# Two-source operations for the softmax factors, and no weight pieces split by GpSimd from the last routing on

## The chip, the core and the metric

The kernel runs on one core of a Trainium2 chip. The core has five engines with a queue of instructions each: TensorE (PE; its weight loads are shown as PEld), VectorE (DVE), ScalarE (ACT), GpSimd (POOL) and SyncE (SP), which here issues most of the DMAs. Each engine takes its instructions in order, and semaphores make one engine wait for another. The metric is the device time of one execution in microseconds (us); the figure of a kernel is the median of its runs.

## The reference

Three layers follow each other in one launch, all in fp32:

```python
attn = rope_attention(q, k, v)        # 2 batches, 8 heads, 576 positions, 64 columns a head
x  = attn as [1152, 512]
p  = domain_probs / (sum + 1e-9)
x1 = sum over 4 experts e of p[:, e] * (relu(x @ w1[e]) @ w2[e])      # every expert on every token
e  = argmax of softmax(norm(x1) . norm(emb) / tau)                    # 8 experts, one per token
out[e == i] = gate * (relu(x1[e == i] @ w1b[i]) @ w2b[i])
```

The attention divides each row of exp(scores - max) by its sum + 1e-9.

## The kernel before

**Precision.** Each fp32 operand of a matmul is held as two float32r tiles, a high part "hi" (a copy that rounds) and a low part "lo" (operand minus hi); a product is three matmuls, hi hi, hi lo and lo hi. So each weight has to be split on the chip, by a copy (hi, normally ScalarE, `L657`, tile `wh`) and a subtraction with two sources in SBUF (lo, `L658`, tile `wl`).

**Attention (0 to about 190 us).** Heads go in eight pairs. `Schedule` orders the operations of all engines in a greedy run over estimated costs and ranks (`POS`), and `ENG` gives the engine of operations that have a choice. For each pair VectorE adds 1e-9 to the row sums (`row_sum`, `L350`, tile `rs`), takes the reciprocal (`L354`), and makes two operands of a small set of matmuls (`rmat`): `mrs` (`rest_factor`, `L359`) and `rb`, the factors spread over 64 columns each (`wide_factor`, `L365`). `rb` is made by GpSimd, for pair 1 by VectorE. Beside them GpSimd does the rotary products (`raw`), low parts of q and k (`n`), of v (`vs`) and of the result (`xl`), all with two sources in SBUF.

**First expert layer (190 to 585 us).** TensorE-bound; weight pieces of 128 x 512 are split between its products.

**Last routing (585 to about 622 us).** Tokens go in nine chunks of 128. `route_one` routes chunks 6, 7 and 8 one after the other: VectorE adds the last expert's sum (`L814`, tile `x`), squares it (`sq`), GpSimd takes the root (`ss`), TensorE transposes and makes the logits, VectorE picks the expert (`lm`, `eq`, `em`, `oh`, then `ss`, `nb`), ScalarE makes the gate (`ex`), and VectorE the slot (`rk`, `slot`, `es`, `seen`). `first_split` puts the 16 pieces of the first block's weights (units 0 to 3, four pieces each) between these steps: hi on ScalarE, and lo on VectorE for the six pieces named in `FIRST_ON_DVE`, on GpSimd for the other ten.

**Second expert layer (to the end).** Fourteen blocks of 128 tokens of one expert. A block has 48 matmuls of 128 x 512 (`fc1` and `fc2`, `L1291`) in four sets of 12, and 12 transposes (`turned`, `L1268`), each four of which need a copy by ScalarE and a subtraction by VectorE (`L1270`: `bxl`, `htl`). Beside them 16 weight pieces are split for the next blocks. Of each unit's four pieces the one numbered 3 has its lo on GpSimd, and for the odd units its hi on VectorE (`L655`); the rest is ScalarE and VectorE. The results leave through an indirect DMA that GpSimd issues (`L1327`).

Of the kernel before, what the change touches and what calls it, by code (L numbers as in the profile page):

```python
# [20 lines left out]
S = 576  # L21
# [7 lines left out]
class Schedule:  # L29
    """Puts operations of several engines in order: a greedy run over estimated costs, in which  # L30
    a free engine takes the operation of the lowest rank among those that can start by then."""
# [7 lines left out]
    def op(self, rank, eng, cost, f, *a, after=(), slot=None, late=0.0):  # L39
        """slot names a buffer of a ring, held from the first operation that names it until all  # L40
        in self.free[slot] are over; late is what the result takes beyond the engine's time."""
        o = dict(rank=rank, eng=eng, cost=cost, f=f, a=a, after=list(after), slot=slot, late=late, end=None)
        self.ops.append(o)
        return o

    def start(self, o, now):
        """When an operation can start, None as long as that is open."""
# [14 lines left out]
    def run(self):  # L62
        """The operations, as dicts, by their start."""
# [32 lines left out]
class Attention:  # L96
    """RoPE attention, two heads at a time; x^T goes to xh + xl (both float32r).

    Round r runs the scores and the softmax of pair r beside the transposes and the
    products with v of pair r - 1, and prepares the operands of pair r + 1.  # L100
    """
# [36 lines left out]
    # engines of the operations that have a choice, pair by pair  # L138
    ENG = {("rope", 0): "gggggggg", ("rope", 1): "gggggggg", ("rope", 2): "vvgggggg", ("split", 0): "aaaaaaaa",
           ("split", 1): "gggggggg", ("v", 0): "aaagaaaa", ("v", 1): "gggggggg", ("wide", 0): "gvgggggg",  # L140
           ("x", 0): "aaaagggg", ("x", 1): "gggggggg", ("rope1q", 0): "ggv", ("rope1k", 0): "vvv",
# [55 lines left out]
    def rope(self, eng, i, j, sl=slice(0, 2), cols=slice(0, S)):  # L197
        """Step j of x * cos + swapped x * sin, in place; slot 0 is q, 1 is k."""
# [18 lines left out]
    def spread(self, i):  # L217
        """qa = [qh; ql] of head A, qb = [ql; qh] of head B, ka and kb = k of a head on both halves."""
# [16 lines left out]
    def first_pair(self, D):  # L235
        """Loads and operands of pair 0, in small parts and without DMAs between partitions;
        what each chunk of its scores waits for."""
# [73 lines left out]
    def qk(self, i, c):  # L311
        """Scores of row chunk c; chunks 0-3 head A, 4 the rests of both, 5-8 head B."""
# [34 lines left out]
    def row_sum(self, i):  # L347
        nc, st = self.nc, self.st[i]
        rs = st["rs"] = self.p_sm.tile([128, 9], F32, name="rs")
        nc.vector.tensor_scalar(out=rs, in0=st["sum"], scalar1=1e-9, scalar2=None, op0=ALU.add)  # L350
# [5 lines left out]
    def rest_factor(self, i):  # L356
        nc, st = self.nc, self.st[i]
        mrs = st["mrs"] = self.p_sm.tile([128, 128], F32, name="mrs")
        nc.vector.tensor_scalar(out=mrs, in0=self.cst["blk"], scalar1=st["rs"][:, 8:9], scalar2=None, op0=ALU.mult)  # L359

    def wide_factor(self, eng, i):
        st = self.st[i]
        rb = st["rb"] = self.p_sm.tile([128, 8, 64], F32, name="rb")
        sh = [128, 8, 64]
        self.by(eng).tensor_tensor(out=rb, in0=self.cst["one"].unsqueeze(2).to_broadcast(sh),  # L365
                                in1=st["rs"][:, 0:8].unsqueeze(2).to_broadcast(sh), op=ALU.mult)
# [46 lines left out]
    def av(self, i, h, hf, k):  # L413
        """One of the five key chunks of x^T; any of them may come first."""
# [11 lines left out]
    def av_shift(self, i, h, hf):  # L426
        """The low half of x^T moves to the rows of the main half."""
# [12 lines left out]
    def rmat(self, i):  # L440
# [5 lines left out]
        nc.tensor.matmul(ps[:, 512:S], st["mrs"], self.cst["id2"], start=True, stop=True)  # L446
# [32 lines left out]
    def plan(self, last_round):  # L479
        """All operations, with what they wait for."""  # L480
# [14 lines left out]
        for i in range(NPAIR):  # L495
            # operands
# [34 lines left out]
            # scores and softmax  # L531
            for c in range(9):
# [11 lines left out]
            f = [op("row_factor", i, 2, "DVE", 128, self.rest_factor, i, after=[f]),  # L544
                 op("row_factor", i, 3, self.letter("wide", 0, i), 400, self.wide_factor, self.letter("wide", 0, i), i,
                    after=[f])]
            # transposes and products with v
# [57 lines left out]
class Experts:  # L605
    """Both expert layers. A weight unit is [128, 2048]: 0 and 1 are the halves of w1's columns
    as [p, k, 512], 2 and 3 the halves of w2's rows as [p, f, 512]; each is held as hi + lo."""
# [6 lines left out]
    FIRST_ON_DVE = (0, 0), (0, 1), (2, 0), (2, 1), (2, 2), (3, 0)  # L614
# [6 lines left out]
    def open_right(self, ctx):  # L621
        """Weights and the first split unit, in place of what the attention no longer needs."""
# [28 lines left out]
    def split(self, cut, u, lo_eng=None, hi_eng=None):  # L651
        nc = self.nc
        raw, hi, lo = cut(self.raw[u]), cut(self.wh[u]), cut(self.wl[u])
        if hi_eng:
            hi_eng.tensor_copy(hi, raw)  # L655
        else:
            nc.scalar.activation(out=hi, in_=raw, func=AF.Copy)  # L657
        (lo_eng or nc.vector).tensor_tensor(out=lo, in0=raw, in1=hi.bitcast(F32), op=ALU.subtract)  # L658

    def split_rows(self, u, j, *engines):  # L660
        self.split(lambda t: t[:, j * 512:(j + 1) * 512], u, *engines)

    def split_cols(self, u, j, *engines):
        self.split(lambda t: t.rearrange("p (a b) -> p a b", b=512)[:, :, j * 128:(j + 1) * 128], u, *engines)

# [18 lines left out]
    def layer1(self, xh, xl, rest):  # L684
        """All but the routing of the last token chunk, which is left in self.todo."""
        tc = self.tc
        with ExitStack() as c1:
# [28 lines left out]
            for c in range(3):  # L716
# [9 lines left out]
                # the first block's weights are split beside the chunk's routing  # L726
# [8 lines left out]
    def first_split(self, u, *js):  # L735
        for j in js:
            self.split_rows(u, j, *[] if (u, j) in self.FIRST_ON_DVE else [self.nc.gpsimd])

# [5 lines left out]
    def next_splits(self, n):  # L744
        """Splits of the weights needed next; a unit's next load follows its split."""
# [71 lines left out]

    def router_setup(self):
# [30 lines left out]
        def scale():  # L849
            """Embeddings over tau (|emb| + 1e-6)."""  # L850
# [11 lines left out]
        def empty():  # L862
            """Empty slots: zero rows whose token lies beyond the output."""
# [15 lines left out]
    def turn(self, c, cols, ps=None):  # L879
        """Part of a chunk's x1^T."""  # L880
# [27 lines left out]
    def counts(self, c, ps=None):  # L908
        """Tokens per expert in the chunks before c, in every partition."""
# [4 lines left out]
    def rank(self, cs):  # L914
        """Slots: the expert's region + tokens before in the chunk + tokens of the chunks before."""
# [8 lines left out]
    def scatter(self, c):  # L924
        # no order among the scatters can be declared between direct neighbours on the engine
# [7 lines left out]
    def route(self, chunks):  # L933
        """Logits and the one-hot of the first largest."""
# [7 lines left out]
        # the sums of the last token block leave half of the accumulators free  # L942
# [34 lines left out]
    def first_block(self):  # L977
        """The expert with the most tokens in the first six chunks comes first, the others follow in turn, and
        the slots of its first block are filled (or left empty) by these chunks alone, so that the second layer
        can start with that block. Then slots and gates of these chunks."""  # L980
# [5 lines left out]
        def choose():  # L986
# [8 lines left out]
            # e1 = the first expert, place = (e - e1) mod 8  # L995
# [9 lines left out]
            # 128 rows of NT / 128 place  # L1005
# [457 lines left out]
```

## Time and profile before

| what | before |
|---|---|
| median of 3 runs | 804.32 us (803.84 to 804.36) |
| profiled execution: span from the first to the last instruction | 802.5 us |
| TensorE busy | 749.2 us, 93% |
| VectorE busy | 490.5 us, 61% |
| ScalarE busy | 377.1 us, 47% |
| GpSimd busy | 252.7 us, 31% |

The trace covers one execution, and its span is 1.8 us shorter than the median of the runs. "Busy" of an engine includes time in which an instruction has started and does not get on. The share of the whole span hides the stages: VectorE is idle in most of the first expert layer, and busy without a gap in the second.

### The profile page before, as it was taken

How to read it: one execution, taken by the hardware profiler on the slowest of the kernel's cores; microseconds unless marked ns; L12 is line 12 of the kernel's file. 1: busy time of each engine (PE TensorE's matmuls, PEld its weight loads, DVE VectorE, ACT ScalarE, POOL GpSimd, SP SyncE). 2: the span in 40 equal slices, each digit the busy share in tenths (PEclk: the TensorE clock that was granted, in tenths of full speed). 3: DMA queues.
4: the chain of work that ended last, by engine and by line, in shares of the span. 5: the costliest groups of instructions: out<-in, count | busy, mean ns of one | idle time of the engine just before them, and what ended most of it. 6: DMA issues, size and time to landing. Idle time of an engine off the chain costs nothing.

```text
span 802.5 us, 11114 instructions
## 1 busy us (share of the span) xinstructions
PE 749.2 (93%) x4002; PEld 653.4 (81%) x4002; DVE 490.5 (61%) x840; ACT 377.1 (47%) x767; POOL 252.7 (31%) x180
## 2 busy tenths in 40 slices
PE   2798888999999999999999999999988799999996
PEld 1687777889999999999999999999966577777775
DVE  7889999997122351222512225232558999999994
ACT  5587888884101231112311123111234788788883
POOL 4777685223100000000000000000084567665662
PEclk9899999999999999999999999999997999999999
DMA  6766664534340089900390000000071265594010
GB/s 200 218 168 162 170 162 89 142 131 185 139 124 0 1 239 313 288 1 1 130 291 0 1 1 1 0 1 1 21 292 43 93 230 206 187 376 155 27 41 17
DMA packets 31837, 97.27 MB, mean 121 GB/s; under 512 B 4638, under 2 KB 6174, under 8 KB 25760
## 3 DMA queue, kind: packets, MB, share of 16 engines
q1 hardware_dynamic: 29936, 91.77, 36.6%
q0 software_dynamic: 1840, 4.73, 1.6%
q8 instruction: 33, 0.54, 0.3%
q14 instruction: 28, 0.23, 0.1%
HBM read 58.32 MB, written 27.09 MB: 106 GB/s over the span
## 4 chain that ended last, share of the span: by engine, by line
PE 58%; DVE 23%; issue 7%; ACT 5%; POOL 3%; SPq 2%; DMA 2%; ACTq 0%; POOLq 0%; DVEq 0%
DVE wl L658 12%; PE ps L788 8%; PE ps L790 8%; PE ps L789 8%; PE acc L806 8%; PE acc L804 8%; PE acc L805 8%; PE av L424 2%; PE sc L327 2%; DVE nm L337 2%; SPq L224 2%; PE psa L1291 1%; ACT wh L657 1%; DVE p L411 1%; ACT e L344 1%
## 5 line engine op out<-in xcount | busy, mean ns | idle before, releaser
L794 DVE SCALAR_TENSOR_TENSOR hl<-ps,hh 128x384 fp32r<-128x384 f32 x96 | 53.5, 558 | 269.6 <-ACT hh L793 269.6
L658 DVE TENSOR_TENSOR wl<-raw,wh 128x512 fp32r<-128x512 f32 x222 | 190.1, 897 | 4.7 <-ACT wh L657 4.7
L793 ACT ACTIVATE hh<-ps 128x384 fp32r<-128x384 f32 x96 | 47.1, 491 | 304.5 <-PE ps L790 302.9
L657 ACT ACTIVATE wh<-raw 128x512 fp32r<-128x512 f32 x258 | 143.1, 627 | 5.2 <-DMA raw<-in_w_dram 2.8
L788 PE MATMUL ps<-xh,wh 128*128 128x384 f32 x384 | 130.3, 339 | 0.0
L790 PE MATMUL ps<-xh,wl 128*128 128x384 f32 x384 | 129.7, 338 | 0.0
L789 PE MATMUL ps<-xl,wh 128*128 128x384 f32 x384 | 129.5, 337 | 0.0
L658 POOL TENSOR_TENSOR wl<-raw,wh 128x512 fp32r<-128x512 f32 x62 | 105.2, 1714 | 49.4 <-DVE wh L655 27.3
L905 POOL TENSOR_TENSOR ss<-ss,half 128x1 f32<-128x1 f32 (+1 forms) x5 | 3.5, 704 | 355.1 <-DVE sq L894 355.1
L806 PE MATMUL acc<-wh,hl 128*128 128x512 f32 x288 | 114.4, 397 | 0.0
L804 PE MATMUL acc<-wh,hh 128*128 128x512 f32 x288 | 114.4, 397 | 0.0
L805 PE MATMUL acc<-wl,hh 128*128 128x512 f32 x288 | 113.7, 395 | 0.0
L789 PEld LDWEIGHTS ps<-xl,wh 128*128 128x128 f32 x384 | 72.2, 188 | 3.9
L788 PEld LDWEIGHTS ps<-xh,wh 128*128 128x128 f32 x384 | 72.2, 188 | 3.8
L790 PEld LDWEIGHTS ps<-xh,wl 128*128 128x128 f32 x384 | 72.1, 188 | 0.0
L806 PEld LDWEIGHTS acc<-wh,hl 128*128 128x128 f32 x288 | 54.2, 188 | 12.5
L805 PEld LDWEIGHTS acc<-wl,hh 128*128 128x128 f32 x288 | 54.2, 188 | 8.8
L804 PEld LDWEIGHTS acc<-wh,hh 128*128 128x128 f32 x288 | 54.1, 188 | 8.3
L344 ACT ACTIVATE e<-sc,nm 128x576 f32<-128x576 f32 x72 | 53.4, 742 | 9.7 <-DVE nm L337 9.4
L337 DVE TENSOR_REDUCE nm<-sc 128x1 f32<-128x576 f32 x72 | 53.8, 750 | 2.8 <-PE sc L327 1.7
L389 PE MATMUL pt<-ident,e 128*128 128x128 f32 (+1 forms) x304 | 47.6, 283 | 7.4 <-DVE ptl L411 6.3
L1291 PE MATMUL pso<-wh,htl 128*128 128x512 f32 x112 | 44.6, 407 | 5.0 <-DVE htl L1270 5.0
(233 smaller groups left out, 1298.9 us busy)
## 6 DMA issues: line engine op xcount, KB each, us to landing
raw<-in_w_dram SPq DMA_DIRECT2D x40, 1024.0 KB, 5.6
xs<-z SPq DMA_DIRECT2D x10, 2056.0 KB, 14.3
raw<-in_qk_dram SPq DMA_DIRECT2D x7, 1152.0 KB, 5.3
ka<-n SPq DMA_DIRECT2D x14, 288.0 KB, 3.9
kb<-n SPq DMA_DIRECT2D x14, 288.0 KB, 4.4
xin<-xs SPq DMA_DIRECT2D x13, 257.0 KB, 4.0
rv<-in_v_dram SPq DMA_DIRECT2D x8, 320.0 KB, 5.4
qa<-n SPq DMA_DIRECT2D x14, 144.0 KB, 4.2
```

What stands on the lines that cost most here:

```text
L337: nc.vector.tensor_reduce(out=st["nm"][:, c:c + 1], in_=st["sc", c][:, :, :SH], axis=AX.XY, op=ALU.max, negate=True)
L344: nc.scalar.activation(out=e.rearrange("p (a b) -> p a b", a=2), in_=st.pop(("sc", c))[:, :, :SH], func=AF.Exp, bias=st["nm"][:, c:c + 1], ...
L657: nc.scalar.activation(out=hi, in_=raw, func=AF.Copy)
L658: (lo_eng or nc.vector).tensor_tensor(out=lo, in0=raw, in1=hi.bitcast(F32), op=ALU.subtract)
L788: nc.tensor.matmul(o, wcut(self.wh[u], k), xh[:, k, cs], start=(k == 0), stop=False)
L789: nc.tensor.matmul(o, wcut(self.wh[u], k), xl[:, k, cs], start=False, stop=False)
L790: nc.tensor.matmul(o, wcut(self.wl[u], k), xh[:, k, cs], start=False, stop=(k == 3))
L794: nc.vector.scalar_tensor_tensor(out=hl, in0=o, scalar=0.0, in1=hh.bitcast(F32), op0=ALU.max, op1=ALU.subtract)
L804: nc.tensor.matmul(acc, hh[:, js], wh, start=(f == 0), stop=False)
L805: nc.tensor.matmul(acc, hh[:, js], wl, start=False, stop=False)
L806: nc.tensor.matmul(acc, hl[:, js], wh, start=False, stop=(f == 7))
L1291: self.nc.tensor.matmul(acc, a[:, k * 128:(k + 1) * 128], w[u][:, k * 512:(k + 1) * 512], start=start, stop=stop)
```

## The change

`row_sum` adds a tile of 1e-9 in place of the constant. `rest_factor` multiplies the 64-column `id2` (two identities side by side, summed) with the factor broadcast to 64 columns, in place of the 128-column `blk` with a factor per partition, and `rmat` multiplies `blk` by that. `wide_factor` is on GpSimd for all eight pairs. The split of weight pieces has no engine to choose any more: from the last routing on, every hi copy is ScalarE's and every lo subtraction VectorE's. (Docstrings and comments go too; they move line numbers by a few.)

```diff
-           ("split", 1): "gggggggg", ("v", 0): "aaagaaaa", ("v", 1): "gggggggg", ("wide", 0): "gvgggggg",
-           ("x", 0): "aaaagggg", ("x", 1): "gggggggg", ("rope1q", 0): "ggv", ("rope1k", 0): "vvv",
+           ("split", 1): "gggggggg", ("v", 0): "aaagaaaa", ("v", 1): "gggggggg", ("x", 0): "aaaagggg", ("x", 1): "gggggggg", ("rope1q", 0): "ggv", ("rope1k", 0): "vvv",
...
-        nc.vector.tensor_scalar(out=rs, in0=st["sum"], scalar1=1e-9, scalar2=None, op0=ALU.add)
+        nc.vector.tensor_tensor(out=rs, in0=st["sum"], in1=self.cst["tiny"], op=ALU.add)
...
-        mrs = st["mrs"] = self.p_sm.tile([128, 128], F32, name="mrs")
-        nc.vector.tensor_scalar(out=mrs, in0=self.cst["blk"], scalar1=st["rs"][:, 8:9], scalar2=None, op0=ALU.mult)
+        mrs = st["mrs"] = self.p_sm.tile([128, 64], F32, name="mrs")
+        nc.vector.tensor_tensor(out=mrs, in0=self.cst["id2"], in1=st["rs"][:, 8:9].to_broadcast([128, 64]),
+                                op=ALU.mult)
...
-        nc.tensor.matmul(ps[:, 512:S], st["mrs"], self.cst["id2"], start=True, stop=True)
+        nc.tensor.matmul(ps[:, 512:S], self.cst["blk"], st["mrs"], start=True, stop=True)
...
-            f = [op("row_factor", i, 2, "DVE", 128, self.rest_factor, i, after=[f]),
-                 op("row_factor", i, 3, self.letter("wide", 0, i), 400, self.wide_factor, self.letter("wide", 0, i), i,
-                    after=[f])]
+            f = [op("row_factor", i, 2, "DVE", 64, self.rest_factor, i, after=[f]),
+                 op("row_factor", i, 3, "POOL", 400, self.wide_factor, i, after=[f])]
...
-    FIRST_ON_DVE = (0, 0), (0, 1), (2, 0), (2, 1), (2, 2), (3, 0)
...
-        if hi_eng:
-            hi_eng.tensor_copy(hi, raw)
-        else:
-            nc.scalar.activation(out=hi, in_=raw, func=AF.Copy)
-        (lo_eng or nc.vector).tensor_tensor(out=lo, in0=raw, in1=hi.bitcast(F32), op=ALU.subtract)
+        nc.scalar.activation(out=hi, in_=raw, func=AF.Copy)
+        nc.vector.tensor_tensor(out=lo, in0=raw, in1=hi.bitcast(F32), op=ALU.subtract)
...
-            self.split_rows(u, j, *[] if (u, j) in self.FIRST_ON_DVE else [self.nc.gpsimd])
+            self.split_rows(u, j)
...
-        self.split_rows(u, j, *([self.nc.gpsimd, self.nc.vector if u % 2 else None] if j == 3 else []))
+        self.split_rows(u, j)
...
+    nc.vector.memset(new("tiny", [128, 9]), 1e-9)
```

In the attention the order of every engine stays as it was but for pair 1. On VectorE, from the row sums of pair 1 on, before (`nm` is the row maximum of the next pair, `ptl` a low part of the transposed exponentials, `t` the result):

```order
L350 TENSOR_SCALAR rs<-sum 128x9
L354 RECIPROCAL rs<-rs 128x9
L337 TENSOR_REDUCE nm<-sc 128x1
L365 TENSOR_TENSOR rb<-one,rs 128x512
L411 TENSOR_TENSOR ptl<-pt,pth 128x512
L337 TENSOR_REDUCE nm<-sc 128x1
L438 TENSOR_TENSOR t<-av_562,t 64x288
L337 TENSOR_REDUCE nm<-sc 128x1
L411 TENSOR_TENSOR ptl<-pt,pth 128x512 x2
L337 TENSOR_REDUCE nm<-sc 128x1
L359 TENSOR_SCALAR mrs<-blk,rs 128x128
L455 TENSOR_TENSOR t<-t,sc 128x576
```

And the same place after the change:

```order
L349 TENSOR_TENSOR rs<-sum,tiny 128x9
L353 RECIPROCAL rs<-rs 128x9
L336 TENSOR_REDUCE nm<-sc 128x1
L358 TENSOR_TENSOR mrs<-id_74,rs 128x64
L411 TENSOR_TENSOR ptl<-pt,pth 128x512
L336 TENSOR_REDUCE nm<-sc 128x1
L438 TENSOR_TENSOR t<-av_564,t 64x288
L336 TENSOR_REDUCE nm<-sc 128x1
L411 TENSOR_TENSOR ptl<-pt,pth 128x512 x2
L336 TENSOR_REDUCE nm<-sc 128x1
L455 TENSOR_TENSOR t<-t,sc 128x576
```

`rb` has left VectorE's line, and `mrs` stands in its place, six operations earlier than it did. On GpSimd `rb` of pair 1 now stands behind that pair's neighbour `n` and ahead of two rotary products.

At the last routing, VectorE's line for chunk 6 and the sum of chunk 7, before:

```order
L1082 RECIPROCAL ss<-ss 128x1
L1084 TENSOR_SCALAR nb<-lm_5169,ss 128x1
L1090 SCALAR_TENSOR_TENSOR rk_5198,sl_5199<-ps,oh 128x8
L1092 CAST slot<-sl_5199 128x1
L1093 TENSOR_SCALAR es_5178<-es_5178 128x1
L1094 RECIPROCAL x_2072<-es_5178 128x1
L1095 TENSOR_TENSOR seen<-seen,oh 128x8
L814 SCALAR_TENSOR_TENSOR x_2072<-acc_5137,p,x_2072 128x256 x2
```

And after:

```order
L1077 RECIPROCAL ss<-ss 128x1
L1079 TENSOR_SCALAR nb<-lm_5171,ss 128x1
L653 TENSOR_TENSOR wl_2221<-raw_2069,wh_2220 128x512 x3
L1085 SCALAR_TENSOR_TENSOR rk_5200,sl_5201<-ps,oh 128x8
L1087 CAST slot<-sl_5201 128x1
L1088 TENSOR_SCALAR es_5180<-es_5180 128x1
L1089 RECIPROCAL x_2074<-es_5180 128x1
L1090 TENSOR_TENSOR seen<-seen,oh 128x8
L809 SCALAR_TENSOR_TENSOR x_2074<-acc_5139,p,x_2074 128x256 x2
```

Three pieces that GpSimd had now stand on VectorE ahead of the slot of chunk 6 and of the sum of chunk 7.

In the second layer, VectorE's line over one block (units 3, 1, 0 and 2 are split in that order), before:

```order
L1270 TENSOR_TENSOR bxl<-ps,bxh 128x512
L1280 CAST btok<-xin 128x1
L658 TENSOR_TENSOR wl_2223<-raw_2069,wh_2222 128x512
L655 CAST wh_2222<-raw_2069 128x512
L658 TENSOR_TENSOR wl_2223<-raw_2069,wh_2222 128x512 x2
L1270 TENSOR_TENSOR htl_5843<-ps,hth_5842 128x512
L1242 UNCONDITIONAL_BRANCH
L658 TENSOR_TENSOR wl_2219<-raw_2067,wh_2218 128x512
L655 CAST wh_2218<-raw_2067 128x512
L658 TENSOR_TENSOR wl_2219<-raw_2067,wh_2218 128x512 x2
```

And after:

```order
L1265 TENSOR_TENSOR bxl<-ps,bxh 128x512
L1275 CAST btok<-xin 128x1
L653 TENSOR_TENSOR wl_2225<-raw_2071,wh_2224 128x512 x4
L1265 TENSOR_TENSOR htl_6161<-ps,hth_6160 128x512
L1237 UNCONDITIONAL_BRANCH
L653 TENSOR_TENSOR wl_2221<-raw_2069,wh_2220 128x512 x4
L1237 UNCONDITIONAL_BRANCH
L1265 TENSOR_TENSOR htl_6195<-ps,hth_6194 128x512
```

For each unit the fourth lo is VectorE's now, and the copies (`L655`) are gone from its line; they have gone to ScalarE. GpSimd is left with the output DMAs alone.

## Rows read from the trace of the kernel before

**Rows 1.** Stages: start:end, length, busy (x instructions) of PE, PEld, DVE, ACT, POOL; clock

```profile
50.00:200.00 150.00, 136.54 (x946) 122.06 (x946) 139.96 (x224) 119.25 (x262) 82.57 (x47) 1.00 0.56 156
600.00:642.00 42.00, 34.62 (x148) 26.16 (x148) 37.25 (x75) 25.86 (x51) 21.78 (x20) 0.88 0.24 81
642.00:782.00 140.00, 137.36 (x653) 109.85 (x653) 140.00 (x197) 115.13 (x217) 90.58 (x55) 1.00 0.49 175
```

**Rows 2.** Same stages, `L658` alone (DVE, POOL), then `L655` alone (DVE)

```profile
600.00:642.00 42.00, 24.29 (x23) 17.29 (x12) 0.88 0.24 81
642.00:782.00 140.00, 116.93 (x132) 76.97 (x44) 1.00 0.49 175
...
642.00:782.00 140.00, 9.13 (x22) 1.00 0.49 175
```

**Rows 3.** `L658` on VectorE, 640 to 780 us: min/median/max ns; two in a row

```profile
L658 DVE TENSOR_TENSOR wl<-raw,wh x131: 674/680/1786, 639.3 to 779.7; 128x512 fp32r<-128x512 f32 x131
...
648.42 1.28 DVE L658 TENSOR_TENSOR wl<-raw,wh 128x512 fp32r<-128x512 f32 x2
```

**Rows 4.** TensorE's timeline over one block: start, length, [idle before it, releaser]

```profile
641.74 0.50 PE L1291 MATMUL pso<-wh,htl 128*128 128x512 f32 x1 [1.32 <-DVE htl L1270]
...
653.80 0.39 PE L1291 MATMUL pso<-wh,hth 128*128 128x512 f32 x1
654.02 0.39 PE L1291 MATMUL pso<-wl,hth 128*128 128x512 f32 x1
654.70 0.50 PE L1291 MATMUL pso<-wh,htl 128*128 128x512 f32 x1 [0.29 <-DVE htl L1270]
```

**Rows 5.** TensorE's waits from 585 us on: us in total, times, longest

```profile
PE ps L921 <- DVE oh L1081: 2.9, 1, 2.9
PE psa L1291 <- DVE wl L658: 2.7, 1, 2.7
PE ps L919 <- ACT ex L1085: 1.8, 1, 1.8
```

**Rows 6.** TensorE's only waits from 642 to 782 us

```profile
PE pso L1291 <- DVE htl L1270: 4.0, 11, 1.3
```

**Rows 7.** The two constant-operand factors in the attention: count, busy us, mean ns

```profile
L359 DVE TENSOR_SCALAR mrs<-blk,rs 128x128 f32<-128x128 f32 x8 | 9.4, 1171 | 0.0
L350 DVE TENSOR_SCALAR rs<-sum 128x9 f32<-128x9 f32 x8 | 8.7, 1091 | 1.0 <-ACT e L344 0.9
```

**Rows 8.** Timeline of VectorE and GpSimd at the factors of pairs 0 and 1

```profile
37.69 1.17 DVE L359 TENSOR_SCALAR mrs<-blk,rs 128x128 f32<-128x128 f32 x1
37.73 1.04 POOL L365 TENSOR_TENSOR rb<-one,rs 128x512 f32<-128x512 f32 x1 [0.36 <-DVE rs L354]
...
58.43 2.66 POOL L187 TENSOR_TENSOR n<-raw,n 128x1152 fp32r<-128x1152 f32 x1 [2.46 <-ACT n L182]
59.06 2.58 DVE L365 TENSOR_TENSOR rb<-one,rs 128x512 f32<-128x512 f32 x1
...
68.31 1.41 POOL L187 TENSOR_TENSOR xl<-t,xh 128x576 fp32r<-128x576 f32 x1 [1.57 <-ACT xh L182]
```

**Rows 9.** Timeline of VectorE, ScalarE and GpSimd in the last routing

```profile
591.59 0.21 DVE L1084 TENSOR_SCALAR nb<-lm,ss 128x1 f32<-128x1 f32 x1
592.19 1.66 ACT L657 ACTIVATE wh<-raw 128x512 fp32r<-128x512 f32 x3
592.67 0.86 DVE L814 SCALAR_TENSOR_TENSOR x<-acc,p,x 128x256 f32<-128x256 f32 x2
593.93 4.22 POOL L658 TENSOR_TENSOR wl<-raw,wh 128x512 fp32r<-128x512 f32 x3
...
608.00 3.20 DVE L658 TENSOR_TENSOR wl<-raw,wh 128x512 fp32r<-128x512 f32 x1 [0.26 <-ACT wh L657]
...
615.94 1.27 POOL L658 TENSOR_TENSOR wl<-raw,wh 128x512 fp32r<-128x512 f32 x1 [1.43 <-ACT wh L657]
616.24 1.01 DVE L1141 SCALAR_TENSOR_TENSOR ctl<-blkno,row 128x17 int32<-128x17 f32 x1
```

More of the change, by code (lines that the diff above doesn't have):

```diff
@@ L357, in rest_factor, with wide_factor @@
         nc, st = self.nc, self.st[i]
-        mrs = st["mrs"] = self.p_sm.tile([128, 128], F32, name="mrs")
-        nc.vector.tensor_scalar(out=mrs, in0=self.cst["blk"], scalar1=st["rs"][:, 8:9], scalar2=None, op0=ALU.mult)
-    def wide_factor(self, eng, i):
+        mrs = st["mrs"] = self.p_sm.tile([128, 64], F32, name="mrs")
+        nc.vector.tensor_tensor(out=mrs, in0=self.cst["id2"], in1=st["rs"][:, 8:9].to_broadcast([128, 64]),
+                                op=ALU.mult)
+    def wide_factor(self, i):
         st = self.st[i]
@@ L364, in wide_factor @@
         sh = [128, 8, 64]
-        self.by(eng).tensor_tensor(out=rb, in0=self.cst["one"].unsqueeze(2).to_broadcast(sh),
-                                in1=st["rs"][:, 0:8].unsqueeze(2).to_broadcast(sh), op=ALU.mult)
+        self.nc.gpsimd.tensor_tensor(out=rb, in0=self.cst["one"].unsqueeze(2).to_broadcast(sh),
+                                     in1=st["rs"][:, 0:8].unsqueeze(2).to_broadcast(sh), op=ALU.mult)
     def pt(self, i, u):
@@ L649, in load1, with split, split_rows, split_cols @@
         self.nc.sync.dma_start(out=self.raw[u], in_=self.w1_d[e * 4 + u])
-    def split(self, cut, u, lo_eng=None, hi_eng=None):
+    def split(self, cut, u):
         nc = self.nc
         raw, hi, lo = cut(self.raw[u]), cut(self.wh[u]), cut(self.wl[u])
-        if hi_eng:
-            hi_eng.tensor_copy(hi, raw)
-        else:
-            nc.scalar.activation(out=hi, in_=raw, func=AF.Copy)
-        (lo_eng or nc.vector).tensor_tensor(out=lo, in0=raw, in1=hi.bitcast(F32), op=ALU.subtract)
[L660 to L664, printed above, removed]
+        nc.scalar.activation(out=hi, in_=raw, func=AF.Copy)
+        nc.vector.tensor_tensor(out=lo, in0=raw, in1=hi.bitcast(F32), op=ALU.subtract)
+    def split_rows(self, u, j):
+        self.split(lambda t: t[:, j * 512:(j + 1) * 512], u)
+    def split_cols(self, u, j):
+        self.split(lambda t: t.rearrange("p (a b) -> p a b", b=512)[:, :, j * 128:(j + 1) * 128], u)
     def open_layer1(self, ctx):
```

## The prediction

> **What bounds the kernel now.** I read the stages first, then in each stage what TensorE waits for. From 642 to 782 us VectorE is busy 140.00 of 140 us, and TensorE 137.36 [rows 1]. TensorE waits there 11 times, each time for VectorE's `htl` [rows 6]. Its stalls repeat: one ends at 641.74, the next at 654.70, so a block takes 12.96 us [rows 4]. VectorE sets this pace, and only just: matmuls of 128 x 512 follow each other at 0.22 to 0.23 us (653.80 and 654.02), while the stalled one starts 0.68 us after its neighbour [rows 4]. Without that wait a block would lose 0.45 us and end at about 12.5 us, and TensorE would be the bound.
>
> Then, what is VectorE doing in its 140 us? 132 lo pieces take 116.93 us [rows 2], 0.89 us each, though the shortest takes 0.674 and the median 0.680 us, and two in a row take 1.28, that is one every 0.60 us [rows 3]. At 0.60 the 132 pieces would be 79.2 us; the other 37.7 us are spent waiting inside the instruction. The long ones overlap GpSimd's pieces. A short case shows it best: `ctl`, a two-source operation of 17 columns, took 1.01 us with a GpSimd piece that had begun 0.30 us before it [rows 9], and ended with that piece (616.24 + 1.01 = 617.25; 615.94 + 1.27 = 617.21). So 44 GpSimd pieces in this stage cost VectorE 37.7 / 44 = 0.86 us each, more than the 0.60 us for which VectorE would do one itself.
>
> **The second layer's steady part.** VectorE takes over 44 pieces: +44 x 0.60 = +26.4. The waiting goes: -37.7. Its 22 hi copies (9.13 us [rows 2]) go to ScalarE: -9.1 at most. Sum -20.4, so about 120 us of VectorE work in place of 140, below TensorE's 137. The gain is then cut off by TensorE: ten blocks (the eleventh wait belongs to the stage before) at 0.45 us give **-4.5 us**. From below: -3, if some blocks still stall where a new expert's weights arrive; from above no more than -4.9, all 11. ScalarE gets 22 copies at 0.52 us (three in a row take 1.66, the first about 0.62 [rows 9]): +11.4 to 126.6 of 140. That costs nothing as long as its own copies for TensorE (`h`, `hth`) stay ahead; the cover is the one phase of 12 matmuls, 2.8 us, between a transpose and its use.
>
> **The last routing and the first block (585 to 642 us).** Here the order matters, since VectorE takes its line in turn.
> - Chunk 6: three pieces now stand between `nb` and the slot. Their hi copies follow `ex` on ScalarE and run from 592.19 to 593.85 [rows 9]; the third lo can begin at about 594.05 and ends at 594.7. The slot's four small operations and the 1.08 us that now pass from `nb` to the sum of chunk 7 (591.59 to 592.67 [rows 9]) come behind that, so the sum starts near 595.5: 2.9 us later. TensorE needs it at once, so it stands that long.
> - Most is given back at once: `ss` of chunk 7 had to wait behind three GpSimd pieces, to 593.93 + 4.22 = 598.15 [rows 9], and TensorE then stood 1.8 us for `ex` [rows 5]. That queue is gone. Net at 600 us: **+1.1**.
> - Chunk 8: the piece at 608.00 took 3.20 us, 2.5 of it waiting, with two GpSimd pieces beside it [rows 9]. TensorE stood 2.9 us for the `oh` behind it [rows 5]. The two pieces move to VectorE, 1.2 us: **-1.3**.
> - `ctl` (1.01 [rows 9]; like small ones 0.21): **-0.8**, on the way to the load of the next block.
> - The 2.7 us for `wl` [rows 5] and the 1.32 us at 641.74 [rows 4] stand behind waiting pieces: in 600 to 642 us, 23 pieces took 24.29 us against 13.8, 10.5 of waiting, and 12 GpSimd pieces come back at 0.60 [rows 2], so VectorE gains 10.5 - 7.2 = 3.3 net, and it has 4.75 us idle besides (42 - 37.25 [rows 1]), most of it waits for work that would itself come earlier. Of the 8 us that both make I have booked 2.1 in the two lines above; I take -2.0 of the 2.7 and all of the 1.3, where the pieces stand closest: **-3.3**.
>
> Sum **-4.3**. It is the least certain term: the granted clock was 0.88 here [rows 1], so TensorE ran about 10 us at the lower of its two levels, 1.2 GHz, after it had stood idle. A longer stall at 593 and shorter ones at 609 and 633 move this stretch; by +-2 us, so -2 to -6.5. What GpSimd keeps (scatters, `ss`) only comes earlier.
>
> **The attention.** All `rs` and `mrs` together take 8.7 + 9.4 = 18.1 us for 16 tiny operations [rows 7], mostly waiting for a GpSimd operation to end. Does the two-source form escape? The nearest row says no: `rb` of pair 1 on VectorE, two sources in SBUF, began at 59.06 and took 2.58 us, to 0.55 us past the end of GpSimd's `n` (58.43 + 2.66 = 61.09) [rows 8]; and `ctl` with 17 columns waited likewise [rows 9]. So I give nothing for the form. What remains: for pair 1 `rb` leaves VectorE, but `mrs` takes its place behind the same `n` and waits to 61.1, 2.1 us instead of 2.58; the `mrs` that stood later (mean 1.17 [rows 7]) is gone: -1.5 or so. On GpSimd `rb` adds 1.04; its idle 1.57 us before 68.31 [rows 8] covers it. For pair 0 `mrs` began 0.04 us ahead of `rb` and lost (1.17) [rows 8]; at best it now wins, -1.0. VectorE is busy 139.96 of 150 us here [rows 1], so most of this arrives: **-1.5**, between 0 and -2.5. The swapped matmul has the same shape: nothing; the fill of `tiny` lies before the first load lands: nothing.
>
> The Trainium skill, "SBUF — State Buffer", section "SBUF: two separate sides", has a rule that speaks against this half of the change: VectorE and GpSimd share a port pair that is locked for a whole instruction, and VectorE takes it in a two-port mode or with two SBUF inputs while a GpSimd operation reads SBUF. By it the new forms wait as the old did, and the trace's `rb` with 2.58 us agrees; the sum by it is the one above.
>
> **Sum.** -4.5 - 4.3 - 1.5 = -10.3 us on the profiled 802.5 us span, so 792.2. The runs' median is 804.32, 1.8 above that span; with the same 1.8, **794.0 us**. By the bounds: -3, -2, 0 to -4.9, -6.5, -2.5, that is 790 to 799.
>
> **Rivals.**
> - *Small two-source operations don't wait.* Then the 18.1 us shrink to 16 x 0.21 = 3.4 [rows 7, 9], 14.7 less on VectorE. TensorE has 13.5 us free in 50 to 200 us [rows 1], so -7 to -13 rather than -1.5: about 784. Against it stands `ctl`. Chance 0.08. The Trainium skill's "Advanced Engine Details and Errata", "VectorE Performance Modes", would give this: it lists no two-port mode for tensor_tensor, and says that two-port instructions and GpSimd's block each other. By that table alone the new forms are free; `rb` in the trace differs.
> - *The routing eats its part.* The stall at chunk 6 is not given back, and the low clock stays: the middle term is 0 and not -4.3, so 798 to 800. For it speaks that VectorE's line now holds what GpSimd did aside. 0.13.
> - *ScalarE becomes the bound (slower).* Place: its line in each block, with two more copies at 0.52. If the 24.9 us that it is idle in 642 to 782 [rows 1] are all waits that can't move, a block takes 12.96 + 1.04 = 14.0 us: 11 x 1.04 = +11.4 in place of -4.5, so about 810. It decides when `h` or `hth` ends later than TensorE's set of 12 matmuls, 2.8 us after the transpose. 0.05.
> - *VectorE's long pieces are not GpSimd's doing (slower).* Then it gets 26.4 us, less 9.1, more in a stage where it is busy all the time [rows 1], and 12 x 0.60 before it: about 825. Against: the minimum and median of 0.674 and 0.680 with a maximum of 1.786 [rows 3]. 0.03.
> - *Nothing comes of it*: block pace set by DMA, routing even: 803 to 805. 0.03.
>
> **How the numbers follow.** My own forecast has 0.68, at 790 to 799; that and the routing case make 0.81 within 790 to 800. I stretch it on the low side by half of the first rival, to 786, and to 801 above. Faster than before by over 0.2% (1.6 us, about what a measurement of this kernel can tell from no change): 0.68 + 0.08 + 0.11 of the 0.13 = 0.87. Within 0.2%: 0.05. Slower: 0.08.
>
> **What would show it.** Right: lo pieces on VectorE at 0.60 to 0.69 us without long ones from 585 us on; 642 us onwards about 12.5 us a block with VectorE near 90% and TensorE's waits for `htl` gone; a stall of about 3 us at the sum of chunk 7, and shorter ones for `oh` and `wl`; `rs` and `mrs` still 1 to 2 us in pairs 2 to 5. Wrong: blocks that stay at 12.96 us, with waits for `hth` or `psa` copies on ScalarE; `rs` at 0.2 us beside a running GpSimd operation; a longer stretch at the lower clock after the stall at 593.

## The result, and the profile after

The changed kernel took 794.35 us (median of 4 runs, 791.35 to 795.47) against 804.16 us of the kernel before beside it: a ratio of 0.9871, 95% interval 0.9858 to 0.9883. The profiled execution has a span of 791.5 us. The forecast, 794.0, is met, but its closeness is luck, for two errors cancel: the split half gave more than forecast, and the attention half made the kernel slower. The parts below take that apart.

The stages after the change, in the columns of [rows 1]; the last two rows are `L653` (the old `L658`) alone, on VectorE:

```profile
50.00:200.00 150.00, 138.01 (x951) 124.41 (x950) 133.85 (x223) 118.91 (x261) 82.12 (x48) 0.99 0.56 155
600.00:642.00 42.00, 37.88 (x183) 28.36 (x183) 37.33 (x96) 31.37 (x63) 5.75 (x9) 1.00 0.33 115
642.00:782.00 140.00, 139.75 (x673) 114.05 (x673) 129.93 (x222) 128.25 (x243) 11.40 (x12) 1.00 0.47 170
...
600.00:642.00 42.00, 24.76 (x40) 1.00 0.33 115
642.00:782.00 140.00, 108.80 (x176) 1.00 0.47 170
```

In the second layer VectorE and TensorE have changed places: VectorE now has 10 us free of 140 and TensorE 0.25. VectorE makes 176 lo pieces there in less time than it took for 132 before [rows 2]. The spread of their durations says why (min/median/max in ns, beside [rows 3]):

```profile
L653 DVE TENSOR_TENSOR wl<-raw,wh x179: 680/684/693, 639.7 to 779.4; 128x512 fp32r<-128x512 f32 x179
```

The median has not moved, and the tail to 1786 ns is gone. At the place in the block where TensorE stood before [rows 4], one block apart:

```profile
649.17 0.39 PE L1286 MATMUL pso<-wl,hth 128*128 128x512 f32 x1
649.40 0.40 PE L1286 MATMUL pso<-wh,htl 128*128 128x512 f32 x1
...
661.60 0.40 PE L1286 MATMUL pso<-wl,hth 128*128 128x512 f32 x1
661.84 0.39 PE L1286 MATMUL pso<-wh,htl 128*128 128x512 f32 x1
```

The matmul on `htl` follows at 0.23 to 0.24 us with no wait, and a block takes 12.44 us (661.84 - 649.40) in place of 12.96. TensorE's waits from 585 us on, in the columns of [rows 5]:

```profile
PE ps L880 <- DVE x L809: 2.3, 2, 1.6
PE ps L916 <- DVE oh L1076: 1.9, 2, 1.2
PE psa L1286 <- ACT bxh L1264: 0.7, 1, 0.7
PE pso L1286 <- DVE htl L1265: 0.5, 1, 0.5
...
PE psa L1286 <- DVE wl L653: 0.2, 1, 0.2
```

The waits for `wl`, `ex` and the eleven for `htl` are gone or small; a new one for `x` (`L809`) heads the list. Its place, on VectorE, ScalarE and TensorE (start, length, [idle before it, releaser]):

```profile
594.12 1.89 DVE L653 TENSOR_TENSOR wl<-raw,wh 128x512 fp32r<-128x512 f32 x3 [1.04 <-ACT wh L652]
595.93 0.16 DVE L1085 SCALAR_TENSOR_TENSOR rk<-ps,oh 128x8 f32<-128x8 f32 x1
...
596.52 0.87 DVE L809 SCALAR_TENSOR_TENSOR x<-acc,p,x 128x256 f32<-128x256 f32 x2
...
593.46 1.66 ACT L652 ACTIVATE wh<-raw 128x512 fp32r<-128x512 f32 x3
...
597.14 0.80 PE L880 MATMUL ps<-ident,x 128*128 128x128 f32 x4 [1.62 <-DVE x L809]
```

Three hi copies on ScalarE, three lo pieces behind them, the slot of chunk 6, the sum of chunk 7, and only then TensorE: the chain that the forecast described.

**Where the time went.** The start of the same matmul in two traces, one subtracted from the other, tells where time is gained or lost. Each column is one kernel's profile minus that of the kernel before, in us, each counted from the start of its own span, at the matmuls that stand at these times before; the last of them is TensorE's last. Where a column falls, the kernel gains; where it is level, the two run at the same pace.

| time before | changed | attention half | split half | blocks alone | routing alone | tile alone |
|---|---|---|---|---|---|---|
| 20.0 | +0.49 | +0.09 | -0.02 | +0.21 | -0.02 | +0.04 |
| 170.0 | -4.93 | -1.67 | +0.05 | +0.58 | +0.44 | +0.10 |
| 186.9 | -1.29 | +0.44 | -0.01 | +0.59 | +0.40 | +0.11 |
| 574.9 | +1.68 | +3.41 | 0.00 | +0.60 | +0.40 | +3.07 |
| 600.0 | +1.94 | +3.43 | +0.22 | +0.57 | +0.60 | +3.09 |
| 641.7 | -4.88 | +2.68 | -5.92 | -2.71 | -2.85 | +3.24 |
| 784.6 | -10.47 | +2.76 | -12.11 | -8.87 | -2.85 | +3.37 |
| 796.9 | -10.93 | +2.88 | -12.68 | -9.47 | -2.86 | +3.48 |

The other columns are the experiments that follow.

### The profile page after: what moved, and what is told of

The parts are those of the page before. It is cut to its first block, busy times and chain, and to the rows that moved or that the text cites. A ratio compares the mean times of both kernels' runs of the same rounds, so it can differ in the third digit from the quotient of the medians.

```text
span 791.5 us, 11019 instructions
## 1 busy us (share of the span) xinstructions
PE 746.6 (94%) x4002; PEld 654.0 (83%) x4002; DVE 465.6 (59%) x876; ACT 389.8 (49%) x793; POOL 145.1 (18%) x119
## 5 line engine op out<-in xcount | busy, mean ns | idle before, releaser
L653 DVE TENSOR_TENSOR wl<-raw,wh 128x512 fp32r<-128x512 f32 x284 | 177.9, 685 | 7.1 <-ACT wh L652 7.1
L652 ACT ACTIVATE wh<-raw 128x512 fp32r<-128x512 f32 x284 | 156.7, 627 | 4.4 <-SPq L1237 2.5
L326 PE MATMUL sc<-ka,qa 128*128 128x288 f32 x160 | 33.5, 330 | 17.2 <-POOL qa L186 15.0
L411 DVE TENSOR_TENSOR ptl<-pt,pth 128x512 fp32r<-128x512 f32 x68 | 45.7, 682 | 2.4 <-ACT pth L407 1.6
```

The lines of the kernel that those rows point to most:

```text
L653: nc.vector.tensor_tensor(out=lo, in0=raw, in1=hi.bitcast(F32), op=ALU.subtract)
```

## The experiments

**The two halves, and the two parts of the split half.** Four kernels, each the kernel before with one part of the change: the attention half; the split half; of the split half `split_piece` alone (the second layer's blocks); and `first_split` alone (the last routing).

The edits of the split half are these two; the blocks alone have the first of them, the routing alone the second, and the attention half all of the diff that isn't here.

```diff
-        self.split_rows(u, j, *([self.nc.gpsimd, self.nc.vector if u % 2 else None] if j == 3 else []))
+        self.split_rows(u, j)
...
-            self.split_rows(u, j, *[] if (u, j) in self.FIRST_ON_DVE else [self.nc.gpsimd])
+            self.split_rows(u, j)
```

> Only the attention half: the two-source forms of rs and mrs, rb of pair 1 on GpSimd, the tile tiny. Theory A (the prediction's own term): the form does not escape GpSimd, the attention gains 1.5 us, nothing else moves: 802.7. Theory B (read from the changed kernel's profile): the attention gains about 5 us by operations that shift against GpSimd's, but 3.4 us go at the seam to the first layer, where a half-clock stretch at 181.8 to 185.2 us appears, and 3.2 us in the first layer, so the sum is +1.7: about 806. Rival (small two-source operations are free): rs and mrs at 0.2 us in all pairs, 790 to 797.

> Only the split half: every lo piece on VectorE and every hi on ScalarE from the last routing on. Theory A (prediction): -4.5 and -4.3, so 795.5. Theory B (the changed kernel's profile, where from 575 us to the end 12.7 us are gained): 791.6, which is better than both halves together. If the halves add to the changed kernel's 794.35 and the attention half alone is slower, B stands; if this kernel is slower than the changed one, A's attention term is real.

> Only split_piece, the second layer's steady part; the last routing keeps its ten GpSimd pieces. Theory: a block takes 12.44 to 12.5 us in place of 12.96, eleven of them, and the stall at 641.74 goes or not: -4.5 to -6.5, so 798 to 800; TensorE's waits for htl between 655 and 782 us gone. Rival (VectorE's long pieces are not GpSimd's doing): blocks get slower, 815 to 825. Rival (ScalarE bound): 14 us a block.

> Only first_split: the ten GpSimd pieces of the last routing go to VectorE; the blocks stay as before. Theory (prediction's middle term): a stall of about 3 us at the sum of chunk 7, given back behind it, -3 to -4.5 in all by 642 us and the same 12.96 us a block behind it: 800 to 801. Read from the changed kernel's profile the stage gained 6.5 us: 798. Rival (the routing eats its part): 804 to 806.

| kernel | median us | ratio to before | 95% interval |
|---|---|---|---|
| attention half | 805.75 | 1.0022 | 1.0003 to 1.0041 |
| split half | 791.90 | 0.9846 | 0.9833 to 0.9858 |
| blocks alone | 794.33 | 0.9870 | 0.9856 to 0.9884 |
| routing alone | 802.34 | 0.9975 | 0.9965 to 0.9985 |

The split half alone is better than both halves together, by about 0.25% (0.9871 against 0.9846; the two intervals touch at 0.9858), and the attention half alone is 0.2% slower. Theory B of the first two expectations stands. The blocks alone give five sixths of the split half (-10.5 of -12.4 us by the ratios, on 804.3), more than any expectation allowed for: its column falls by 3.3 us between 600 and 641.7 already, since the pieces of the first blocks start there, by 6.2 more to 784.6, and by 0.6 in the last block. The routing alone gives 3.5 us between 600 and 641.7 and nothing behind, and 2.0 us by the ratio, less than the 800 to 801 us expected; its blocks keep the long pieces:

```profile
L658 DVE TENSOR_TENSOR wl<-raw,wh x130: 674/679/1787, 640.5 to 778.9; 128x512 fp32r<-128x512 f32 x130
```

**Where the attention half loses.** Two kernels: the kernel before with `tiny` filled and never read, and the kernel before with `rb` of pair 1 on GpSimd.

```diff
+    nc.vector.memset(new("tiny", [128, 9]), 1e-9)
...
-("wide", 0): "gvgggggg"
+("wide", 0): "gggggggg"
```

> The kernel before with the 36-byte tile tiny filled at the start and never read; nothing else changed. It moves every tile that is allocated behind it by 36 bytes a partition. Theory (the place of the tiles makes the first layer's matmuls slower): the first layer loses about 3 us between 190 and 575 us as in the changed kernel and in the kernel with the attention half alone, so 807.5. Rival (the loss comes from what the attention half does, not from the tile): 804.5, no drift in the first layer.

> Only rb of pair 1 moved from VectorE to GpSimd, with the old forms of rs and mrs. Theory (placement, not form, is what moves the attention): the attention gains 1.5 to 3 us by 125 us, as with the whole attention half, without the drift of the first layer: 802 to 803. Rival (the forms do it): no gain, 804.5.

The tile alone took 807.02 us, ratio 1.0035 (1.0023 to 1.0048): slower by 2.8 us, for 36 bytes that nobody reads. Its column is level but between 186.9 and 574.9 us, where it loses 2.96 us; the changed kernel and the attention half lose 2.96 and 2.97 there. All five kernels with the tile lose 2.96 to 2.97 us in that stretch, and in the kernels without it that stretch changes by at most 0.06. The loss is spread evenly over the first layer. 200 to 580 us in the kernel with the split half alone, then in the kernel with the tile alone:

```profile
200.00:580.00 380.00, 380.00 (x1950) 345.02 (x1949) 112.83 (x227) 73.76 (x146) 5.05 (x10) 1.00 0.26 81
```

```profile
200.00:580.00 380.00, 380.00 (x1934) 344.31 (x1933) 110.33 (x212) 73.23 (x145) 5.04 (x10) 1.00 0.26 81
```

TensorE is busy throughout and at the full granted clock in both, but in the same 380 us it issues 16 of 1950 matmuls fewer, 0.8%, which is 3 us. The instructions of the layer are the same. What the tile can change for them is where their operands lie in SBUF; that is concluded by exclusion, since no run moved the operands in another way.

`rb` of pair 1 alone took 804.93 us, ratio 1.0013 (1.0004 to 1.0023). That misses the expected 802 to 803. Its trace was 3.2 us ahead at 95.0 us, 1.1 us behind at 110.0 and 170.0, and 3.1 us behind at 186.9, with no drift in the first layer. The 4.2 us between 95 and 110 us were lost around a stretch in which TensorE's granted clock was at 1.2 GHz, 97.3 to 104.1 us; the kernel before has no such stretch between 34.7 and 601.3 us. And 2.1 us are lost between the attention and the first layer, as with the attention half (2.1). TensorE there, in the kernel before and then in the changed one:

```profile
183.28 0.29 PE L424 MATMUL av<-ptl,vs 128*128 128x288 f32 x1
183.41 0.34 PE L788 MATMUL ps<-xh,wh 128*128 128x384 f32 x1
```

```profile
178.36 0.29 PE L424 MATMUL av<-ptl,vs 128*128 128x288 f32 x1
180.52 0.42 PE L783 MATMUL ps<-xh,wh 128*128 128x384 f32 x1 [1.87 <-DVE t L455]
...
181.86 0.52 PE L784 MATMUL ps<-xl,wh 128*128 128x384 f32 x1
```

Before, the first layer starts at once. After the change its first matmul waits 1.87 us for `t` of the last pair, although it reads nothing of it. The order of the program shows the wait, in the same row of TensorE's line, before and after:

```
675 L788 MATMUL ps<-xh,wh_2070 128x384
675 L783 MATMUL ps<-xh,wh_2072 128x384 [waits DVE_49,PE_49]
```

The wait comes with the move of `rb`: the traces of all four kernels with the move have it, and those of the kernel before and of the forms alone (below) don't. Its reason is read from the program and not varied by a run: the two PSUM buffers of the attention's scores alternate, and with `rb` of pair 1 moved they come in the other order, so that the last `sc`, which `L455` still reads, lies in the bank that the first layer's `ps` takes. In the changed kernel's profile TensorE's granted clock fell, after this stop of 1.87 us, to the lower of its two levels, 1.2 GHz, from 181.8 to 185.2 us (the 384-column matmul at 181.86 takes 0.52 us), and the seam cost 3.6 us in all. In the profiles of the attention half and of `rb` alone, with a stop of 1.9 us, the clock stayed at 2.4 GHz there and the seam cost 2.1.

**The forms, and the tile in another size.** Two kernels with `tiny` as the first nine columns of a 16-column tile: the whole change, and the kernel before with the new forms of `rs` and `mrs` only.

```diff
-    nc.vector.memset(new("tiny", [128, 9]), 1e-9)
+    nc.vector.memset(new("tiny_pad", [128, 16]), 1e-9)
+    cst["tiny"] = cst["tiny_pad"][:, 0:9]
```

> The changed kernel with tiny as the first 36 of 64 bytes, so that the tiles behind it move by 64 bytes and not by 36. Theory (the loss in the first layer comes from where the tiles lie relative to some power of two, not from one more tile): the drift of 3.0 us between 190 and 575 us goes, and the part of it that shows in the second layer's products (0.236 in place of 0.231 us) too: 790.5 to 791.5. Rival (any shift does it): 794.3, drift as before.

> The kernel before with the two-source forms of rs and mrs, tiny as part of 64 bytes, and rb of pair 1 still on VectorE; the split of weights as before. Theory A (the forms wait for GpSimd as the old ones): 803.5 to 804.5, rs and mrs at 1 to 2 us where a GpSimd operation runs. Rival (the forms escape): rs and mrs at 0.2 us throughout, 795 or less. If the sum of the attention half's parts without the shift of the tiles is a gain (805.75 - 3.2 = 802.5), the forms must give it, since rb of pair 1 alone gave 804.9.

The whole change gave 792.96 us, ratio 0.9871 (0.9854 to 0.9889), as without the wider tile, and lost the same 2.97 us in the first layer. This run did not test what it was meant to: by the addresses in both compiled programs the tile takes the same room, so everything behind it lies in the same place. Which displacement is harmless stays open.

The forms alone gave 804.22 us, ratio 1.0008 (0.9995 to 1.0021). Without the tile's 1.0035 that is a gain of 2.2 us, with an interval of 1.4 us either way. So a gain of the forms is likely, but its size is uncertain by more than half. They do not escape GpSimd. Durations of `rs` and `mrs` over the eight pairs (min/median/max in ns), the forms alone, then the changed kernel:

```profile
L350 DVE TENSOR_TENSOR rs<-sum,tiny_pad x8: 159/1002/2018, 36.3 to 175.2; 128x9 f32<-128x9 f32 x8
L359 DVE TENSOR_TENSOR mrs<-id,rs x8: 215/652/1454, 37.7 to 178.4; 128x64 f32<-128x64 f32 x8
```

```profile
L349 DVE TENSOR_TENSOR rs<-sum,tiny x8: 159/170/2009, 37.5 to 170.2; 128x9 f32<-128x9 f32 x8
...
L358 DVE TENSOR_TENSOR mrs<-id,rs x8: 215/1140/2334, 38.2 to 173.5; 128x64 f32<-128x64 f32 x8
```

Nine columns still take up to 2.0 us. In the changed kernel at pairs 1 and 3, on VectorE and GpSimd:

```profile
57.98 2.65 POOL L186 TENSOR_TENSOR n<-raw,n 128x1152 fp32r<-128x1152 f32 x1 [2.46 <-ACT n L181]
58.61 2.10 DVE L358 TENSOR_TENSOR mrs<-id,rs 128x64 f32<-128x64 f32 x1
...
93.78 2.65 POOL L186 TENSOR_TENSOR n<-raw,n 128x1152 fp32r<-128x1152 f32 x1 [3.96 <-ACT n L181]
94.46 2.00 DVE L349 TENSOR_TENSOR rs<-sum,tiny 128x9 f32<-128x9 f32 x1 [0.23 <-ACT e L343]
```

Each began inside GpSimd's `n` and ended with it (58.61 + 2.10 = 60.71 against 60.63; 94.46 + 2.00 = 96.46 against 96.43). In which pairs this happens differs between kernels: the kernel with `rb` moved and the old forms has an `rs` of 0.17 us in pair 2, where before it was 1.88. With the forms alone all `mrs` together take 4.9 us in place of 9.4, since fewer of them meet a GpSimd operation or meet it late; all `rs` take 8.5 in place of 8.7.

What the attention gains by 170 us can't be read off one profile of each kernel: 5.4 us in the changed kernel's, 1.8 with the attention half alone, nothing with the forms alone. The first two run the same attention. Up to 97 us their profiles keep the same distance; they part between 97 and 101 us (1.5 us) and between 114 and 125 us (2.2 us). There the profile of the attention half has TensorE's granted clock at 1.2 GHz, from 98.4 to 101.8 and from 118.8 to 122.3 us, and the changed kernel's has 2.4 GHz. TensorE had waited alike before the first of these stretches, in the attention half and then in the changed kernel (the matmul that follows takes 0.56 and 0.40 us):

```profile
98.28 0.56 PE L425 MATMUL av<-p,vs 128*128 128x288 f32 x1 [0.72 <-DVE p L412]
```

```profile
98.70 0.40 PE L424 MATMUL av<-p,vs 128*128 128x288 f32 x1 [0.72 <-DVE p L411]
```

The profile of the forms alone has four such stretches of 3.4 us between 62 and 145 us. So it doesn't show that the forms gain nothing, and how much of the gain is the forms' and how much comes from moving `rb` stays open. The runs of these kernels spread widely: 803.3 to 811.7 us with the attention half, 803.2 to 808.0 with the forms (whose profiled run, at 806.9, is one of the long ones); that the clock makes this spread too is likely and not shown, since one run of each has a trace.

**Does GpSimd's operation hold VectorE, and which kind does?** Three kernels with the split half alone, in which GpSimd does one more operation per unit into a tile that nobody reads; VectorE's work stays the same.

```diff
         self.split_rows(u, j)
+        if j == 3:
+            cut = lambda t: t[:, 1536:2048]
+            raw, hi = cut(self.raw[u]), cut(self.wh[u]).bitcast(F32)
+            self.nc.gpsimd.tensor_tensor(out=self.aside, in0=raw, in1=hi, op=ALU.subtract)
```

In place of the last line the second kernel has a copy, `tensor_copy(self.aside, hi)`, and the third a fill, `memset(self.aside, 0.0)`.

> The kernel with the split half alone, and in the second layer GpSimd repeats the subtraction of each piece 3 into a tile that nobody reads. VectorE still makes all lo pieces, so nothing waits for GpSimd's result but the next load of the unit. Theory (a two-source VectorE operation stands while GpSimd's two-source operation runs): each of the four extra operations per block costs VectorE 0.86 us, its 11.6 us per block become 15.0, so a block takes about 15 us in place of 12.4 and the kernel 815 to 822; lo pieces with a maximum above 1.7 us. Rival (the long pieces came from something else, such as the order of the pieces or the loads): 792, as without the extra operations.

> As the kernel in which GpSimd repeats the subtraction of each piece 3 into a tile that nobody reads, but with a copy of the hi part, one source in place of two. Theory A (any GpSimd operation that goes over SBUF makes the two-source operation on VectorE stand): as there in proportion to the copy's length; at about 0.6 us against 1.55 us some 800 to 808. Theory B (only two-source GpSimd operations do it): 792, lo pieces with no long ones.

> As that one, but GpSimd fills the tile with zeros, no source. Theory A (any GpSimd operation that goes over SBUF): long lo pieces here too, and some us above 791.9. Theory B (only GpSimd operations that read): 792, lo pieces at 0.68 us throughout.

The subtraction gave 824.74 us (ratio 1.0262, 1.0245 to 1.0280; 815 to 822 had been expected), the copy 794.61 and the fill 792.43 (2 runs each), beside 791.90 without. Lo pieces and GpSimd's operation in 642 to 782 us, with the stage's row of [rows 1], for subtraction, copy and fill:

```profile
642.00:782.00 140.00, 123.83 (x578) 96.52 (x577) 140.00 (x191) 112.94 (x213) 74.37 (x49) 1.00 0.49 173
L658 DVE TENSOR_TENSOR wl<-raw,wh x153: 673/680/2237, 641.9 to 781.3; 128x512 fp32r<-128x512 f32 x153
L1263 POOL TENSOR_TENSOR aside<-raw,wh 128x512 f32<-128x512 f32 x39 | 60.3, 1546 | 45.5 <-ACT wh L657 35.4 <-issue 8.8 <-POOL aside L1263 0.9
...
689.66 0.69 ACT L1331 ACTIVATE by<-pso,xin 128x512 f32<-128x512 f32 x1 [2.42 <-PE pso L1296]
704.39 0.69 ACT L1331 ACTIVATE by<-pso,xin 128x512 f32<-128x512 f32 x1 [2.39 <-PE pso L1296]
```

```profile
642.00:782.00 140.00, 139.13 (x670) 113.14 (x668) 138.30 (x222) 128.61 (x243) 52.94 (x58) 1.00 0.46 170
L658 DVE TENSOR_TENSOR wl<-raw,wh x176: 670/679/1101, 642.4 to 780.7; 128x512 fp32r<-128x512 f32 x176
L1263 POOL COPY aside<-wh 128x512 f32<-128x512 f32 x46 | 39.7, 862 | 66.6 <-ACT wh L657 66.2
```

```profile
642.00:782.00 140.00, 139.75 (x676) 114.56 (x675) 130.05 (x222) 128.27 (x243) 34.77 (x56) 1.00 0.47 170
L658 DVE TENSOR_TENSOR wl<-raw,wh x176: 679/684/693, 642.1 to 778.7; 128x512 fp32r<-128x512 f32 x176
L1263 POOL MEMSET aside<- 128x512 f32 x44 | 23.6, 536 | 1.8
```

With the subtraction the long pieces are back, VectorE is busy 140.00 of 140 us, and a block takes 14.73 us (704.39 - 689.66). Without it VectorE works 129.05 of 140 us in blocks of 12.38 us, 11.41 us a block; the difference of 3.32 us is four operations at 0.83 us each, beside the 0.86 that the forecast read off the trace of before. The copy costs (138.30 - 129.05) / 140 x 12.38 / 4 = 0.20 us each and makes no piece longer than 1.10 us; the fill costs 0.02, and no piece is longer than 0.693. So in these three kernels VectorE is held by the operations with which GpSimd reads SBUF, with two sources far more than with one, and not by the one that only writes. Here the Trainium skill, "SBUF — State Buffer", section "SBUF: two separate sides", says the same as the fill and the subtraction: VectorE with two SBUF inputs is blocked only against a GpSimd operation that reads SBUF, and for the whole instruction. The longest piece beside the subtraction, 2.237 us, agrees with a whole instruction of 1.546 us waited for (0.68 + 1.546 = 2.23). The copy does not: it takes 862 ns, but no piece beside it exceeds 1.10 us, where 0.68 + 0.86 = 1.54 would be possible, and it costs 0.20 us on average. Here the measurement decides.

**A better order for chunk 6.** The split half alone, with the three pieces that stand ahead of chunk 7's sum moved into chunk 7.

```diff
-                between = [[(0, 0), (0, 3)], [(0, 1)], [(0, 2)], [(1, 0)], [(1, 1)], [(1, 2)]], [[(1, 3)]], [
+                between = [[(0, 0), (0, 3)], [(0, 1)], [(0, 2)]], [[(1, 0)], [(1, 1)], [(1, 2)], [(1, 3)]], [
```

> The kernel with the split half alone, and the three pieces that stood between the choice and the slots of chunk 6 moved to chunk 7, two before its choice and one behind it. Theory (TensorE's stall of 2.2 us at the sum of chunk 7 is made by VectorE's line, in which these pieces stand ahead of that sum): most of the stall goes, nothing comes later, so 1.5 to 2 us better than 791.9: 790. Rival (the stall only moves to the choice or the first block's operand): 791.5 to 792.5.

It gave 791.83 us, ratio 0.9847 (0.9831 to 0.9864): no better than without (0.9846). In its trace the stall at chunk 7's sum is indeed gone: against the split half it gains 2.0 us by 597 us. 1.1 us of that are given back by 606 us, behind the moved pieces, and 0.7 won again by 642. TensorE's waits there:

```profile
PE ps L921 <- DVE oh L1081: 1.9, 2, 1.2
PE ps L885 <- DVE x L814: 1.0, 1, 1.0
PE psa L1291 <- ACT bxh L1269: 0.8, 1, 0.8
PE ps L919 <- ACT ex L1085: 0.6, 1, 0.6
```

The 2.3 us for `x` have become 1.0, and waits for `bxh` and `ex` on ScalarE have come up. A net 1.6 us remain in this one profile, which was 1.0 us behind at 20 us already; the medians do not tell the two kernels apart.

## Why the prediction came out right, step by step

- **"VectorE sets this pace ... without that wait a block would lose 0.45 us".** Right in mechanism, and the wait went as foretold. The size was off: a block lost 0.52 us in the changed kernel (12.96 to 12.44) and 0.57 in the kernels without the tile's shift. The stalled matmul itself came 0.41 us earlier; the one behind it gained another 0.11, since after a stop TensorE's first matmul takes 0.34 us to the next and not 0.23 (784.22 to 784.56 us in the trace of before). I had priced the first gap alone, and ten blocks where eleven stalled up to 784.6 us and the last block gained too: -5.6 from 641.7 to 784.6 us instead of -4.5, and -6.2 with the split half alone, with 0.5 and 0.6 more in the last block.
- **"44 GpSimd pieces cost VectorE 0.86 us each".** Shown: putting such operations back costs 0.83 each. VectorE is at 129.93 of 140 and not at about 120: 140 us now hold 11.3 blocks and not 10.8, which makes 125 of 120, and a piece takes 108.80 / 176 = 0.62 us and not 0.60, another 3; the last 2 us I have not traced. ScalarE came to 128.25, with 126.6 foretold; TensorE's waits for it are 0.3 us in that stage, so it is no bound.
- **The last routing, -4.3.** The order of events was right, piece by piece: the stall at chunk 7's sum (2.2 us in place of 2.9), given back by 600 us (+0.26 net there, +1.1 foretold), and gains behind it. The step that was mis-sized is the last one, "-3.3" for the stalls for `wl` and `htl`, and "-1.3" for chunk 8: 585 to 641.7 us gave -6.6 in the changed kernel, -5.9 with the split half alone. The pieces of `first_split` alone gave -3.2 there and the blocks' own pieces alone -3.3; I had cut the sum of both short. Part of it may be TensorE's clock, whose granted mean rose from 0.88 to 1.00 in 600 to 642 us (0.96 with the split half alone); with the blocks alone it stayed at 0.88 and that 3.3 us came all the same.
- **The attention, -1.5.** "I give nothing for the form" was right in its reason: the two-source forms wait as the old ones did, up to 2.0 us for nine columns, and the rival of -7 to -13 us falls. That the forms gain no time is not shown; by the ratios, with the tile's loss taken off, they gain about 2.2 us. The sign of the half was wrong, by two terms left out: "the fill of `tiny` lies before the first load lands: nothing" looked at the time of the fill and not at what the tile does to the first layer, and the tile cost 2.8 us; and for `rb` of pair 1 I asked which operations wait inside the attention, and not what its move does at the end, where 2.1 us went. The wait can be read in the compiled order of TensorE's line. Less these two, the half gains about 3 us (1.8 - 2.8 - 2.1 by the ratio and the trace), within an uncertainty of about that size. A third thing had no term either: in the attention TensorE's granted clock falls in some profiles and not in others, and two profiles of the same attention lie 3.7 us apart, lost around such stretches.
- **The sum.** -4.5, -4.3 and -1.5 made -10.3; the parts run alone made -12.4 and +1.8, together -10.6, and the changed kernel -10.4. That the sum came out within half a microsecond is luck: the split half gave 3.6 us more than its two terms, and the attention half took 3.3 us more than its own. The range and the chances rested on the middle term as the least certain one; the largest error lay in the attention's, whose uncertainty I had put at a microsecond.

What stays open: whether it is the shift of the operands in SBUF by which the tile makes TensorE's matmuls 0.8% slower in the first layer, why, and which shifts do so; why the clock fell after the seam's wait in the changed kernel's profile and not in three others with the same wait, and inside the attention in some profiles and not in others; and what the new forms alone are worth. A kernel with the attention half that neither moves the tiles nor swaps the PSUM buffers wasn't tried. The best of the kernels measured is the split half alone, at 791.9 us (with the reordered pieces 791.8).

## What to carry to other kernels

Work given to GpSimd as help is not free for VectorE: a two-source subtraction of 1.55 us there cost VectorE 0.83 us, more than the 0.62 us that VectorE needs to do it itself, so where VectorE is the bound, take the piece back and look at the whole line again, since the bound then passes to TensorE. Price an edit also by what it moves: run a change's small tile alone, look where the clock fell before two profiles are compared, and compare the waits in the compiled order at the seams between stages. And when a forecast is met, run its halves alone, for the terms may be wrong in opposite directions.

## What was not expected of the hardware

A 36-byte tile that nothing reads made the first layer 0.8% slower (1934 matmuls in place of 1950 in 380 us, both at the granted clock 1.00), presumably by the place of the tiles behind it. Of two profiles with the same attention and the same waits of 0.8 and 0.7 us before 99 us, one had TensorE's granted clock fall to 1.2 GHz there and the other did not. GpSimd's fill of 128 x 512 (0.54 us) holds VectorE not at all, its copy a little (0.20 us), its two-source operation most (0.83 us).
